# Relu, gate arithmetic and a small product on GpSimd, and a new planned order, in a memory-attention kernel followed by two MLPs

## The chip, the cores and the metric

The kernel runs on one core of one Trainium2 chip. The metric is the device time of one execution in microseconds. The core's engines are TensorE (PE, with its weight loads as PEld), VectorE (DVE), ScalarE (ACT), GpSimd (POOL) and SyncE (SP, which here issues the DMAs). Each engine takes its own queue in the order of the program and waits on semaphores of the others.

## What is computed

```python
def phi(x):
    return np.where(x > 0, x, np.exp(x) - 1.0) + 1.0
# B, H, S, D = 4, 8, 576, 64
a = softmax(causal(q @ k.T / 8)); local = a @ v
mem_out = (phi(q) @ M_prev) / (phi(q) @ z_prev + 1e-6)
g = 1.0 / (1.0 + np.exp(-beta))                 # one per head
x = (g * mem_out + (1 - g) * local)             # to 2304 x 512
h = x @ w_in;   x = (h * tanh(softplus(h))) @ w_out       # 512 -> 2048 -> 512
h = x @ w_in2;  out = (h * sigmoid(h)) @ w_out2
```

All in float32; the weights of the two MLPs come in as float64 and are brought to float32 bit by bit on the chip.

## The kernel before

**Stages.** Heads are taken two at a time: 16 pairs, each with 576 tokens of two heads. A pair has the scores (`s4` to `s0` on PE, blocks of query rows), their masked minimum on DVE (`r..`, line 588), the exponentials on ACT (`e..`, line 615), transposes on PE (`X1`, `X2`, `X3`, `W`, line 486) that ACT and DVE copy out of PSUM (lines 476 and 479), and the products with v and the memory (`Vhi`, `Vlo`, line 692), which DVE scales into `xT` (line 696). Then the two MLPs run over `xT` in 32 visits (a quarter of the hidden units by a block of tokens); their products are PE lines 1000 to 1002 and 1068, with seven products where eight would be usual and each factor split into a high and a low part.

**phi and its use.** For each pair `phu` (line 507, ACT) makes relu(q) in tile `u`, `phn` (line 505, POOL) makes q - relu(q) in `e`, `phe` (506, ACT) its exponential, `phf` (508, POOL) adds the two. `phz` and `phy` (509 and 512, POOL) multiply by z, `phr` (513, DVE) sums over the features into `c`, `phg` (516 and 517, POOL) and `phd` (519, DVE) turn that into the memory's factors, `phq` (520, DVE) multiplies 8 of them by the softmax's row sums `z`, and `phmh`, `phml`, `phm0` (534 and 539, POOL) scale phi by them. `za`, `zd`, `zg`, `n00` (641 to 647, on POOL and DVE) treat the row sums.

**The gate.** `exp` on ACT (line 434), five small operations on DVE (437 to 441), then three kinds of copies on ACT (446 to 452). Once per execution.

**Weights.** A decode job is a load into `stg`, then `abs`, `b0`, `b1`, `b2`, `b3` on 512 columns (lines 804 to 821, DVE but for the first jobs' `abs` on ACT); `hi` and `lo` parts and the sums for the seven products follow. For the first half of the first quarter of hidden units POOL does the subtractions (lines 847, 866, 869).

**The order.** The program doesn't issue these steps in the order of loops. `Steps.plan` is a list scheduler: every step has an engine, a planned duration, its predecessors, a due time, and the buffers that it takes and gives back. It runs a clock, lets each free engine take the ready step with the least lateness, and the order in which it starts them is the order in which the program issues them. `SHIFT` is a table of numbers, one for each kind of step, that are added to the due times; the change calls this "order sought", so they come from a search. So a change of a planned duration or of `SHIFT` moves instructions on every queue, SP's loads among them, without changing one of them.

Of the kernel before, what the change touches and what calls it, by code (L numbers as in the profile page):

```python
# [36 lines left out]
class Steps:  # L37
# [3 lines left out]
    def __init__(self):  # L41
        self.ops = {}
        self.cap = {}
        self.takes, self.gives = {}, {}
        self.order_of = {}
        self.after = {}
        self.lag = {}
        self.cols = {}
        self.shift = {}
        self.mode = {}  # L50

# [21 lines left out]
    def plan(self):  # L73
# [44 lines left out]
        mode = 0  # L118
        passed = {}
        self.start = {}  # L120
        order = []
        while done < len(ops):
# [6 lines left out]
            for e in engs:  # L129
# [3 lines left out]
                while ready[e]:  # L133
# [22 lines left out]
                    if k in self.cols:  # L156
                        cycles, count = self.cols[k]
                        if passed.get(int(now / TICK) - 1, 0.0) < BUSY:
                            d = max(d, cycles / 1200.0)
                        t = now  # L160
                        while t < now + d - 1e-9:
                            q = int(t / TICK + 1e-9)
                            b = min(now + d, (q + 1) * TICK)
                            passed[q] = passed.get(q, 0.0) + count * (b - t) / d
                            t = b
                    self.start[k] = now
# [92 lines left out]
def pair_steps():  # L259
# [4 lines left out]
    E("phu", "A", 0.58, ["ldnq"])  # L264
    E("phn", "G", 1.37, ["phu"])
    E("phe", "A", 0.58, ["phn"])
    E("phf", "G", 1.37, ["phe", "phu"])
# [10 lines left out]
    for i in (4, 3, 2, 1):  # L278
# [17 lines left out]
        if i == 1:  # L296
# [7 lines left out]
            E("phq", "D", 0.12, ["za", "phd"])  # L304
# [34 lines left out]
class Attn:  # L339
# [89 lines left out]
    def gates(self):  # L429
# [5 lines left out]

        def sig():
            nc.vector.tensor_scalar(bt, bt, 1.0, None, op0=ALU.add)
            nc.vector.reciprocal(self.g, bt)
            nc.vector.tensor_scalar(self.g1, self.g, -1.0, 1.0, op0=ALU.mult, op1=ALU.add)
            nc.vector.tensor_scalar(self.g1c, self.g1, 1e-20, None, op0=ALU.max)  # L440
            nc.vector.tensor_tensor(self.btg, self.g1c, bt, op=ALU.mult)
# [11 lines left out]
        return exp, sig, spread  # L453
# [40 lines left out]
    def steps(self, p):  # L494
# [10 lines left out]
        f["phn"] = lambda: nc.gpsimd.tensor_tensor(self.get(p, "e"), s["nq"], s["u"], op=ALU.subtract)  # L505
        f["phe"] = lambda: nc.scalar.activation(s["e"], s["e"], AF.Exp)
        f["phu"] = lambda: nc.scalar.activation(self.get(p, "u"), s["nq"], AF.Relu)
# [4 lines left out]
        f["phy"] = lambda: nc.gpsimd.tensor_tensor(s["u"][:, 8], s["e"][:, 8], self.bt[b]["y"][:, hp], op=ALU.mult)  # L512
# [7 lines left out]
        f["phq"] = lambda: nc.vector.tensor_tensor(s["c"][:, :8], s["c"][:, :8], s["z"][:, :8], op=ALU.mult)  # L520
# [184 lines left out]
    def register(self, m):  # L705
        m.cap.update({"A." + r: c for r, c in self.RINGS.items()})
        m.cap.update({"A." + r: t[4] for r, t in self.TILES.items()})
        exp, sig, spread = self.gates()
        m.add(("gate", "exp"), "A", 0.2, [], exp, 25.0, 5.2)
        m.add(("gate", "sig"), "D", 1.0, [("gate", "exp")], sig, 26.0)  # L710
        m.add(("gate", "spread"), "A", 1.0, [("gate", "sig")], spread, 28.0)
# [54 lines left out]
def ps2(n):  # L766
    return 0.126 + n / 960
# [6 lines left out]
class Weights:  # L774
# [104 lines left out]
    def register(self, m, due, last1, last2):  # L879
        m.cap.update({"W.raw": 2, "W.val": self.VALS})  # L880
        for n, job in enumerate(JOBS):
# [5 lines left out]
            slow = 0.05 if first else 0.0  # L887
            for x, e, d, deps in (("ld", "S", 2.2, []), ("abs", "A", 0.53, ["ld"]) if first else ("abs", "D", 0.465, ["ld"]),
                                  ("b0", "D", 0.465, ["abs"]), ("b1", "D", 0.465, ["b0"]), ("b2", "D", 0.735, ["b1"]),
                                  ("b3", "D", 0.735, ["b2"])):  # L890
                m.add(J(x), e, d + (slow if e == "D" else 0.0), [J(y) for y in deps], f[x], t,
# [10 lines left out]
        for ph in range(2):  # L902
            for pr in range(NF // 2):
# [5 lines left out]
                d2 = lambda n: 0.25 + n / 480 if g == "G" else dve(n)  # L909
# [16 lines left out]
class Moe:  # L926
# [169 lines left out]
    def register(self, m, base, ends):  # L1096
# [38 lines left out]
        for n, ((ph, tp), vs, kind) in enumerate(run):  # L1135
# [5 lines left out]
            if kind == "comp":  # L1141
# [10 lines left out]
                mk = lambda x, e, d, deps, at: m.add(K(x), e, d, deps, f[x], at - 2.0)  # L1152
                mk("T1", "D", D2, [K("l11")], min(need["T1"], need["T2"]))
# [32 lines left out]
        for v, (ph, g, tp) in enumerate(VISITS):  # L1186
            w = TBS[tp]
            for c in range(2):
# [13 lines left out]
                act2 = lambda n, ps: (0.17 if ps else 0.212) + n / 1200  # L1202
# [48 lines left out]
    ('gate', 'exp'): -1546.35, ('gate', 'sig'): -1000.81, ('gate', 'spread'): -1110.7, ('a', 'ldkT'): -1506.04,  # L1251
# [219 lines left out]
```

## Time and profile before

| | us |
|---|---|
| three executions | 950.07, 951.50, 951.98 (median 951.5) |
| span of the profiled execution, first to last instruction | 949.0 |
| PE busy in it | 921.2 (97%) |
| DVE busy | 662.5 (70%) |
| ACT busy | 498.9 (53%) |
| POOL busy | 140.4 (15%) |

The profile is of one execution. Its own device time isn't listed apart from the span; the three listed times lie 1.1 to 3.0 us over the span. Busy shares are means over stages that differ: POOL's 140 us all lie in the first fifth.

### The profile page before, as it was taken

Reading aid. Unit: us, or ns where it says so; the run is one execution under the profiler, and the core shown is the slowest. Engines: PE = TensorE matmul, PEld = TensorE weight load, DVE = VectorE, ACT = ScalarE, POOL = GpSimd, SP = SyncE. Lnnn points to the kernel's source line nnn. Section 1 sums busy time; section 2 is a strip of 40 time slices with the busy share of each in tenths; the row PEclk is TensorE's granted clock in tenths of the full one; section 3 lists DMA queues with packets and bytes.
Section 4 is the critical chain, followed back from the end, with each engine's and each line's share of the span. In section 5 each row is a group of like instructions: output and inputs, shape, how many; then the busy total and the mean of one; then the engine's idle time right before and its main releaser. Section 6 shows DMA issues by size and latency. Waiting matters only on the chain.

```text
span 949.0 us, 17264 instructions
## 1 busy us (share of the span) xinstructions
PE 921.2 (97%) x6544; PEld 813.1 (86%) x6544; DVE 662.5 (70%) x1504; ACT 498.9 (53%) x1172; POOL 140.4 (15%) x223
## 2 busy tenths in 40 slices
PE   4989999999999999999999999999999999999998
PEld 2656666799999999999999999998999888989986
DVE  4899899988984558665957889766647765754333
ACT  5998899876654243433433647554533442433330
POOL 5688798300000000000000000000000000000000
PEclk9999999999999999999999999999999999999999
DMA  6546563666647403850375535704550374024412
GB/s 209 149 158 194 165 199 121 213 261 235 221 150 250 156 1 98 274 156 1 117 253 197 221 119 198 278 23 162 189 177 10 108 265 145 1 93 147 157 54 99
DMA packets 60034, 147.72 MB, mean 156 GB/s; under 512 B 7600, under 2 KB 25136, under 8 KB 59952
## 3 DMA queue, kind: packets, MB, share of 16 engines
q1 hardware_dynamic: 59808, 146.30, 45.4%
q8 instruction: 51, 0.84, 0.4%
q10 hardware_dynamic: 144, 0.33, 0.1%
q14 instruction: 31, 0.25, 0.1%
HBM read 108.79 MB, written 37.81 MB: 154 GB/s over the span
## 4 chain that ended last, share of the span: by engine, by line
PE 85%; DVE 4%; ACT 3%; POOL 3%; issue 2%; DMA 2%; SPq 0%; DVEq 0%; POOLq 0%
PE acc L1068 42%; PE psX L1000 7%; PE psX L1001 7%; PE psX L1002 7%; PE psY L1000 4%; PE psY L1001 4%; PE psY L1002 4%; DVE sm L588 2%; PE psW L1001 2%; PE psW L1002 2%; PE psW L1000 2%; PE ps_t L692 2%; PE ps_s L595 2%; PE ps_t L486 1%; ACT Ph L615 1%
## 5 line engine op out<-in xcount | busy, mean ns | idle before, releaser
L1068 PE MATMUL acc<-g,w 128*128 128x320 f32 (+1 forms) x1152 | 218.3, 337 | 0.0
L1068 PE MATMUL acc<-w,g 128*128 128x512 f32 x864 | 214.4, 394 | 0.0
L1068 PEld LDWEIGHTS acc<-g,w 128*128 128x128 f32 x1152 | 183.8, 188 | 13.1
L1068 PEld LDWEIGHTS acc<-w,g 128*128 128x128 f32 x864 | 157.8, 188 | 30.5
L1031 ACT COPY vt<-psX 128x256 f32<-128x256 f32 (+1 forms) x192 | 75.2, 398 | 154.8 <-PE psX L1002 146.0
L1089 DVE TENSOR_TENSOR xT<-acc,xT 128x512 f32<-128x512 f32 (+1 forms) x126 | 77.2, 613 | 93.8 <-PE acc L1068 92.9
L1041 DVE TENSOR_TENSOR g<-vt,g 128x512 fp32r<-128x512 f32 (+1 forms) x128 | 94.1, 754 | 35.4 <-ACT g L1040 34.7
L1029 DVE TENSOR_TENSOR vt<-psY,vt 128x256 f32<-128x256 f32 (+1 forms) x128 | 57.9, 456 | 87.1 <-ACT vt L1031 46.2
L1040 ACT CAST g<-vt 128x512 fp32r<-128x512 f32 (+1 forms) x128 | 83.4, 672 | 31.5 <-PE acc L1068 30.1
L1000 PE MATMUL psX<-x,w 128*128 128x320 f32 (+1 forms) x256 | 75.8, 296 | 0.0
L1001 PE MATMUL psX<-x,w 128*128 128x320 f32 (+1 forms) x256 | 75.7, 296 | 0.0
L1002 PE MATMUL psX<-x,w 128*128 128x320 f32 (+1 forms) x256 | 75.6, 295 | 0.0
L595 PE MATMUL ps_s<-kT,qT 64*128 64x288 f32 (+3 forms) x320 | 66.8, 480 | 6.3 <-DMA kT<-in_kT_dram 4.6
L1037 ACT ACTIVATE vt<-vt 128x640 f32<-128x640 f32 (+1 forms) x64 | 43.8, 685 | 51.8 <-DVE vt L1029 51.5
L588 DVE CUSTOM_DVE_ANT_0 sm<-ps_s,mask 128x288 f32<-128x288 f32 (+3 forms) x128 | 56.9, 472 | 5.4 <-PE ps_s L595 3.1
L1035 ACT ACTIVATE vt<-vt 128x256 f32<-128x256 f32 (+1 forms) x64 | 28.5, 445 | 59.7 <-DVE vt L1029 59.7
L1036 ACT ACTIVATE vt<-psX 128x256 f32<-128x256 f32 (+1 forms) x64 | 26.0, 407 | 50.2 <-PE psX L1002 50.1
L1029 DVE TENSOR_TENSOR vt<-psW,vt 128x256 f32<-128x256 f32 (+1 forms) x64 | 29.1, 455 | 31.7 <-PE psW L1002 31.2
L1000 PEld LDWEIGHTS psX<-x,w 128*128 128x128 f32 x256 | 48.2, 188 | 2.0 <-issue 0.2
L1001 PEld LDWEIGHTS psX<-x,w 128*128 128x128 f32 x256 | 48.3, 189 | 1.7
L875 ACT CAST w<-val 128x512 fp32r<-128x512 f32 (+1 forms) x64 | 34.8, 567 | 26.5 <-DVE val L866 13.1
L1002 PEld LDWEIGHTS psX<-x,w 128*128 128x128 f32 x256 | 48.3, 188 | 0.0
(126 smaller groups left out, 2019.1 us busy)
## 6 DMA issues: line engine op xcount, KB each, us to landing
stg<-in_moe_w_in_dram SPq DMA_DIRECT2D x32, 512.0 KB, 5.6
stg<-in_moe_w_out_dram SPq DMA_DIRECT2D x32, 512.0 KB, 3.5
x<-sp SPq DMA_DIRECT2D x18, 640.0 KB, 4.2
x<-sp SPq DMA_DIRECT2D x18, 512.0 KB
sp<-x SPq DMA_DIRECT2D x12, 640.0 KB, 2.9
sp<-x SPq DMA_DIRECT2D x12, 512.0 KB, 4.1
nv<-in_v_dram SPq DMA_DIRECT2D x16, 320.0 KB, 4.3
x1T<-sp01T SPq DMA_DIRECT2D x8, 640.0 KB
```

What stands on the lines that cost most here:

```text
L588: nc.vector.tensor_tensor_reduce(out, ps, mask, -0.125, init, ALU.add, ALU.min, acc)
L595: nc.tensor.matmul(ps, lhsT=s["qT"][R[j], qcols(i)], rhs=s["kT"][R[j], k0 + cols.start:k0 + cols.stop], start=True, stop=True)
L1000: nc.tensor.matmul(o, lhsT=W(0, kc), rhs=X(0, kc), start=(n in (1, 2, 7) and kc == 0), stop=False, skip_group_check=True)
L1001: nc.tensor.matmul(o, lhsT=W(0, kc), rhs=X(1, kc), start=False, stop=False, skip_group_check=True)
L1002: nc.tensor.matmul(o, lhsT=W(1, kc), rhs=X(0, kc), start=False, stop=(kc == 1), skip_group_check=True)
L1029: nc.vector.tensor_tensor(o, self.bank[q, to], o, op=ALU.add)
L1031: f[f"s{n}"] = lambda n=n: nc.scalar.copy(val(*at[n]), self.bank[q, "X"])
L1037: f["m2"] = lambda: nc.scalar.activation(val(1), val(1), fn)
L1040: f[f"h{c}"] = lambda c=c: nc.scalar.copy(hi(c), val(c))
L1041: f[f"l{c}"] = lambda c=c: nc.vector.tensor_tensor(self.gt(q, c)[:, 1, :2 * tb], val(c), hi(c).bitcast(F32), op=ALU.subtract)
L1068: nc.tensor.matmul(y, lhsT=a, rhs=b, start=(c == 0 and k == 0), stop=(c == 1 and k == 5))
L1089: nc.vector.tensor_tensor(part, acc, part, op=ALU.add)
```

## The change

Per pair: relu goes to POOL as a `max` with 0; `phn` becomes a `min` with 0 of q itself, so that it no longer waits for relu; `phq` goes from DVE to POOL. Of the gate's five operations on DVE only the reciprocal stays there, the others go to POOL. In the planner, a POOL step and a DVE step of the set `lock` now wait for each other (`lock` holds the decode steps on DVE and the subtractions that split the MLPs' inputs), some planned durations are smaller, and the table `SHIFT` is another one throughout.

```diff
+                    if e == "D" and k in self.lock:
+                        d += max(0.0, port["G"] - now)
+                        port["D"] = now + d
+                    if e == "G":
+                        d += max(0.0, port["D"] - now)
+                        port["G"] = now + d
...
-    E("phu", "A", 0.58, ["ldnq"])
-    E("phn", "G", 1.37, ["phu"])
+    E("phn", "G", 0.9, ["ldnq"])
     E("phe", "A", 0.58, ["phn"])
+    E("phu", "G", 0.9, ["ldnq"])
...
-            E("phq", "D", 0.12, ["za", "phd"])
+            E("phq", "G", 0.22, ["za", "phd"])
...
+        def one():
+            nc.gpsimd.tensor_scalar(bt, bt, 1.0, None, op0=ALU.add)
         def sig():
-            nc.vector.tensor_scalar(bt, bt, 1.0, None, op0=ALU.add)
             nc.vector.reciprocal(self.g, bt)
-            nc.vector.tensor_scalar(self.g1, self.g, -1.0, 1.0, op0=ALU.mult, op1=ALU.add)
-            nc.vector.tensor_scalar(self.g1c, self.g1, 1e-20, None, op0=ALU.max)
-            nc.vector.tensor_tensor(self.btg, self.g1c, bt, op=ALU.mult)
+        def rest():                # the same three on nc.gpsimd
...
-        f["phn"] = lambda: nc.gpsimd.tensor_tensor(self.get(p, "e"), s["nq"], s["u"], op=ALU.subtract)
+        f["phn"] = lambda: nc.gpsimd.tensor_scalar(self.get(p, "e"), s["nq"], 0.0, None, op0=ALU.min)
-        f["phu"] = lambda: nc.scalar.activation(self.get(p, "u"), s["nq"], AF.Relu)
+        f["phu"] = lambda: nc.gpsimd.tensor_scalar(self.get(p, "u"), s["nq"], 0.0, None, op0=ALU.max)
-        f["phq"] = lambda: nc.vector.tensor_tensor(s["c"][:, :8], s["c"][:, :8], s["z"][:, :8], op=ALU.mult)
+        f["phq"] = lambda: nc.gpsimd.tensor_tensor(s["c"][:, :8], s["c"][:, :8], s["z"][:, :8], op=ALU.mult)
...
-    ... "abs", "D", 0.465 ... "b0" 0.465, "b1" 0.465, "b2" 0.735, "b3" 0.735 (+ 0.05 for the first jobs)
+    ... "abs", "D", 0.335 ... "b0" 0.335, "b1" 0.335, "b2" 0.6, "b3" 0.6, all in m.lock
...
 SHIFT = {                       # every number another
-    ('gate', 'exp'): -1546.35, ('gate', 'sig'): -1000.81, ('gate', 'spread'): -1110.7,
+    ('gate', 'exp'): -2090.82, ('gate', 'one'): 3021.36, ('gate', 'sig'): 731.24, ('gate', 'rest'): 1.31,
```

## Rows read from the trace of the kernel before

**Rows 1.** Busy time by stage (windows): length, then each engine's, PEclk, DMA, GB/s.
```profile
core 0: us, PE busy (x) PEld busy (x) DVE busy (x) ACT busy (x) POOL busy (x), PEclk, DMA share, GB/s
...
14.00:182.00 168.00, 156.43 (x1815) 105.70 (x1816) 152.50 (x544) 154.26 (x472) 132.05 (x208) 0.98 0.52 163
78.00:80.00 2.00, 2.00 (x20) 1.34 (x20) 2.00 (x5) 0.62 (x3) 1.83 (x3) 0.50 0.50 192
106.00:108.00 2.00, 2.00 (x18) 1.17 (x16) 1.44 (x4) 1.66 (x4) 1.75 (x5) 0.50 0.92 217
182.00:946.00 764.00, 762.52 (x4724) 706.11 (x4722) 506.94 (x956) 341.13 (x694) 1.80 (x1) 1.00 0.44 152
```
**Rows 2.** What PE waited for, whole span (waits): us in total, times, longest.
```profile
PE ps_s L634 <- DVE m L588: 7.8, 2, 7.6
PE ps_s L595 <- DMA kT<-in_kT_dram: 4.6, 1, 4.6
```
**Rows 3.** The first 15 us (timeline): start, length, instruction.
```profile
4.05 0.60 SPq L461 DMA_DIRECT2D nq<-in_q_dram  x1
...
4.65 2.29 PE L595 MATMUL ps_s<-kT,qT 64*128 64x288 f32 x8 [4.65 <-DMA kT<-in_kT_dram]
...
6.15 0.68 ACT L507 ACTIVATE u<-nq 128x576 f32<-128x576 f32 x1 [3.92 <-DMA nq<-in_q_dram]
...
10.08 0.68 ACT L507 ACTIVATE u<-nq 128x576 f32<-128x576 f32 x1 [3.25 <-DMA nq<-in_q_dram]
10.66 0.19 ACT L434 ACTIVATE bt<-bt 128x8 f32<-128x8 f32 x1
...
10.84 1.40 POOL L505 TENSOR_TENSOR e<-nq,u 128x576 f32<-128x576 f32 x1 [2.47 <-ACT u L507]
10.89 1.37 DVE L437 TENSOR_SCALAR bt<-bt 128x8 f32<-128x8 f32 x1 [10.03 <-ACT bt L434]
...
13.98 0.46 DVE L588 CUSTOM_DVE_ANT_0 sm<-ps_s,mask 128x288 f32<-128x288 f32 x1
```
**Rows 4.** A relu on ACT and the instruction after it (timeline).
```profile
23.41 0.68 ACT L507 ACTIVATE u<-nq 128x576 f32<-128x576 f32 x1
...
23.98 0.78 ACT L615 ACTIVATE Ph<-sm,m 128x576 f32<-128x576 f32 x1
```
**Rows 5.** DVE from 14 to 182 us by shape (groups): busy, mean ns, idle before.
```profile
L520 DVE TENSOR_TENSOR c<-c,z 128x8 f32<-128x8 f32 x16 | 7.1, 444 | 0.0
L821 DVE SCALAR_TENSOR_TENSOR val<-stg,val 128x512 uint32<-128x512 uint32 x7 | 6.3, 896 | 0.1
L814 DVE TENSOR_SCALAR val<-val 128x512 f32<-128x512 f32 x8 | 6.0, 754 | 1.7 <-ACT val L804 1.7
```
**Rows 6.** The same lines on DVE from 182 to 946 us, where POOL is idle (groups).
```profile
L821 DVE SCALAR_TENSOR_TENSOR val<-stg,val 128x512 uint32<-128x512 uint32 x57 | 38.7, 685 | 0.5
...
L814 DVE TENSOR_SCALAR val<-val 128x512 f32<-128x512 f32 x56 | 24.2, 441 | 0.5
```
**Rows 7.** Line 520 alone: ns shortest, median, longest (source).
```profile
L520 DVE TENSOR_TENSOR c<-c,z x16: 101/298/1201, 24.3 to 174.8; 128x8 f32<-128x8 f32 x16
```
**Rows 8.** POOL's groups over the whole span: busy, mean ns, idle before.
```profile
L505 POOL TENSOR_TENSOR e<-nq,u 128x576 f32<-128x576 f32 x16 | 22.8, 1422 | 6.5 <-ACT u L507 6.2
...
L517 POOL TENSOR_TENSOR c<-c,bt 128x9 f32<-128x9 f32 x16 | 3.3, 204 | 1.3
...
L420 POOL TENSOR_SCALAR_AFFINE_SELECT smask<-smask 64x64 f32<-64x64 f32 x2 | 0.5, 234 | 0.1
...
L413 POOL TENSOR_SCALAR_AFFINE_SELECT mask<-mask 128x128 f32<-128x128 f32 x1 | 0.3, 292 | 0.1
```
**Rows 9.** POOL's two kinds of tensor_scalar: ns shortest, median, longest (source).
```profile
L516 POOL TENSOR_SCALAR c<-c x16: 201/202/569, 20.7 to 170.2; 128x9 f32<-128x9 f32 x16
L647 POOL TENSOR_SCALAR P<-P,r,g1s x16: 440/452/964, 24.5 to 175.0; 128x128 f32<-128x128 f32 x16
```
**Rows 10.** What POOL waited for from 14 to 182 us (waits).
```profile
POOL e L508 <- ACT e L506: 11.6, 7, 2.9
...
POOL P L647 <- DVE c L520: 3.8, 5, 1.2
```
**Rows 11.** The end of the attention stage (timeline): POOL's last step, the first MLP matmul.
```profile
177.07 1.28 POOL L847 TENSOR_TENSOR w<-val,w 128x512 fp32r<-128x512 f32 x1
...
181.64 0.39 PE L1000 MATMUL psX<-x,w 128*128 128x256 f32 x1
```
**Rows 12.** Decode steps on DVE back to back (timeline).
```profile
188.06 0.42 DVE L806 TENSOR_SCALAR val<-stg 128x512 uint32<-128x512 uint32 x1
188.40 0.68 DVE L818 SCALAR_TENSOR_TENSOR val<-stg,val 128x512 uint32<-128x512 uint32 x1
189.00 0.81 DVE L964 TENSOR_TENSOR x<-xT,x 128x640 fp32r<-128x640 f32 x1
```

More of the change, by code (lines that the diff above doesn't have):

```diff
@@ L50, in __init__ @@
         self.mode = {}
+        self.lock = set()
     def add(self, name, eng, dur, deps, fn, due, after=0.0, lag=0.0, cols=None):
@@ L118, in plan @@
         mode = 0
+        port = {"D": 0.0, "G": 0.0}
         passed = {}
@@ L434, in exp @@
             nc.scalar.activation(bt, bt, AF.Exp, scale=-1.0)
+        def one():
+            nc.gpsimd.tensor_scalar(bt, bt, 1.0, None, op0=ALU.add)
         def sig():
-            nc.vector.tensor_scalar(bt, bt, 1.0, None, op0=ALU.add)
             nc.vector.reciprocal(self.g, bt)
-            nc.vector.tensor_scalar(self.g1, self.g, -1.0, 1.0, op0=ALU.mult, op1=ALU.add)
-            nc.vector.tensor_scalar(self.g1c, self.g1, 1e-20, None, op0=ALU.max)
-            nc.vector.tensor_tensor(self.btg, self.g1c, bt, op=ALU.mult)
+        def rest():
+            nc.gpsimd.tensor_scalar(self.g1, self.g, -1.0, 1.0, op0=ALU.mult, op1=ALU.add)
+            nc.gpsimd.tensor_scalar(self.g1c, self.g1, 1e-20, None, op0=ALU.max)
+            nc.gpsimd.tensor_tensor(self.btg, self.g1c, bt, op=ALU.mult)
         def spread():
@@ L452, in spread @@
                 nc.scalar.copy(self.g1s[r, :], gv[r, j, :])
-        return exp, sig, spread
+        return exp, one, sig, rest, spread
     def load(self, p, nm, queue=None):
@@ L511, in steps @@
             self.bt[b]["z"][:, h0:h0 + 2, :].unsqueeze(1).to_broadcast([P, 4, 2, D]), op=ALU.mult)
-        f["phy"] = lambda: nc.gpsimd.tensor_tensor(s["u"][:, 8], s["e"][:, 8], self.bt[b]["y"][:, hp], op=ALU.mult)
+        f["phy"] = lambda: nc.gpsimd.tensor_tensor(self.get(p, "u")[:, 8], s["e"][:, 8], self.bt[b]["y"][:, hp], op=ALU.mult)
         f["phr"] = lambda: nc.vector.tensor_reduce(out=self.get(p, "c"), in_=s["u"], axis=AX.X, op=ALU.add)
@@ L707, in register @@
         m.cap.update({"A." + r: t[4] for r, t in self.TILES.items()})
-        exp, sig, spread = self.gates()
+        exp, one, sig, rest, spread = self.gates()
         m.add(("gate", "exp"), "A", 0.2, [], exp, 25.0, 5.2)
-        m.add(("gate", "sig"), "D", 1.0, [("gate", "exp")], sig, 26.0)
-        m.add(("gate", "spread"), "A", 1.0, [("gate", "sig")], spread, 28.0)
+        m.add(("gate", "one"), "G", 0.2, [("gate", "exp")], one, 25.5)
+        m.add(("gate", "sig"), "D", 0.12, [("gate", "one")], sig, 26.0)
+        m.add(("gate", "rest"), "G", 0.6, [("gate", "sig")], rest, 27.0)
+        m.add(("gate", "spread"), "A", 0.75, [("gate", "rest")], spread, 28.0)
         for p in range(B * NP):
@@ L766, in ps2 @@
 def ps2(n):
-    return 0.126 + n / 960
+    return 0.07 + n / 960
 def sb1(n):
@@ L886, in register @@
             first = self.first(job)
[L887 to L891, printed above, removed]
+            for x, e, d, deps in (("ld", "S", 2.2, []), ("abs", "A", 0.57, ["ld"]) if first else ("abs", "D", 0.335, ["ld"]),
+                                  ("b0", "D", 0.335, ["abs"]), ("b1", "D", 0.335, ["b0"]), ("b2", "D", 0.6, ["b1"]),
+                                  ("b3", "D", 0.6, ["b2"])):
+                if e == "D":
+                    m.lock.add(J(x))
+                m.add(J(x), e, d, [J(y) for y in deps], f[x], t,
                       lag=1.6 if x == "ld" else 0.0, after=20.0 + 20.0 * n if first and x == "ld" else 0.0)
@@ L908, in register @@
                 g = "G" if ph == 0 and pr < GC // 2 else "D"
-                d2 = lambda n: 0.25 + n / 480 if g == "G" else dve(n)
+                d2 = lambda n: 0.18 + n / 480 if g == "G" else dve(n)
                 t = max(due[a], due[b])
@@ L1152, in register @@
                 mk = lambda x, e, d, deps, at: m.add(K(x), e, d, deps, f[x], at - 2.0)
+                m.lock.update(K(x) for x in ["l" + x for x in XOPS] + ["T1", "T2", "T3", "T4"])
                 mk("T1", "D", D2, [K("l11")], min(need["T1"], need["T2"]))
@@ L1201, in register @@
                     last1.setdefault((ph, pr), []).append(N(n))
-                act2 = lambda n, ps: (0.17 if ps else 0.212) + n / 1200
+                act2 = lambda n, ps: (0.067 if ps else 0.108) + n / 1200
                 e = due[N(4)] + 4.0
@@ L1250 @@
 SHIFT = {
-    ('gate', 'exp'): -1546.35, ('gate', 'sig'): -1000.81, ('gate', 'spread'): -1110.7, ('a', 'ldkT'): -1506.04,
[100 rows of a table removed]
+    ('gate', 'exp'): -2090.82, ('gate', 'one'): 3021.36, ('gate', 'sig'): 731.24, ('gate', 'rest'): 1.31,
[93 rows of a table added]
 }
```

193 rows, old and new, of the table SHIFT are left out of this document.

## The prediction

> **What bounds the kernel now.** I first read the page's slices and then cut the span at the stages. [...] So the span is the attention stage, some 182 us, plus a fixed 764 us, plus 3 us for the last drain and store. What the attention stage gives up, the kernel gives up one for one.
>
> The second reading is that stage. From 14 to 182 us, 168 us, DVE is busy 152.5 (91%), ACT 154.3 (92%), POOL 132.1 (79%), and PE 156.4 (93%) [rows 1]. [...] No engine is alone the bound: four queues run almost full, and each waits a little for the others. Relief of one of them is worth less than its own time.
>
> The third is the start. Of what PE waited for, the two longest entries are one wait of 7.6 us before line 634 for DVE, and the first load [rows 2]. The timeline shows why: PE has its first scores by 4.65 + 2.29 = 6.94 us, but DVE takes up the first of them only at 13.98. Until then DVE stands at the gate's first operation, which waits for ACT's `exp` at 10.66, which stands in ACT's queue behind the relu of pair 1, which waits for its q until 10.08 (its load was issued at 4.05). Then the gate's five operations take 3.1 us, since the first, on 8 elements, takes 1.37 us beside POOL's 1.40 us line 505 [rows 3].
>
> **The change part by part.**
>
> ACT loses 16 relus. One is 0.68 us long, but the next instruction on ACT starts 23.98 - 23.41 = 0.57 us after it [rows 4], so 16 x 0.57 = 9.1 us leave ACT's queue.
>
> DVE loses 16 times line 520, mean 444 ns, 7.1 us busy [rows 5]. It works on 8 elements and takes 101 ns at its shortest, 1201 at its longest [rows 7]; the rest is a wait inside the instruction. Taking 0.07 us off each for the overlap with its follower, 16 x 0.374 = 6.0 us leave DVE's queue.
>
> DVE's decode steps show the same wait: line 814 takes 754 ns in this stage against 441 where POOL is idle, line 821 896 against 685 [rows 5, 6]. With lines 816 and 818, which lie between them, I put the 29 such steps of the stage at about 29 x 0.22 = 6.4 us of waiting. The new planner knows of it and may place them better, but POOL also gets more to do. Bounds: 6.4 us gained, or 1 lost (POOL's busy share rises from 79% to at most 151 / 164 = 92%, and this waiting by the same sixth); I take 1.5 gained. The planner's new durations (0.335 and 0.60) are nearer to the chip than the old 0.465 and 0.735: the decode steps start 0.34 and 0.60 us apart [rows 12].
>
> [...]
>
> POOL loses 16 x 1.42 = 22.8 us of `phn` [rows 8], and gets 32 one-input operations on 576 elements, 16 `phq` and four gate operations. `phq` and a gate operation have their like in line 517, 0.20 us on 9 elements [rows 8]: 20 x 0.21 = 4.2 us. The one-input operation isn't in this trace at that size. From below: the affine select takes 234 ns on 64 and 292 on 128 elements [rows 8], which goes on to 0.292 + 448 x 0.00091 = 0.70 us. From above: line 647, a tensor_scalar with two operands per partition, takes 452 ns on 128 against 202 for line 516 on 9 [rows 9], 2.1 ns an element, which goes on to 1.39 us, as dear as a two-input operation (1.42). I take 0.9, the planner's number, since constants instead of operands per partition make it more like the select. Then POOL's work is 140.4 - 22.8 + 28.8 + 4.2 = 150.6 us; with 0.70 it is 144.2, with 1.39 it is 166.3.
>
> [...]
>
> Waits that go: `phn` no longer stands behind relu on another engine (6.2 us of POOL's idle time [rows 8]); relu can now fill the gap in which POOL waits for the exponential (11.6 us), and POOL no longer waits for line 520 (3.8 us) [rows 10]. These 21.6 us of idle time are what lets POOL carry 10 us more. Waits that come: the relus and `phq` now stand in POOL's queue ahead of `phf`, `phz` and the scaling, and PE's transposes `W` and `X3` wait for that scaling.
>
> The lock terms, the durations and `SHIFT` change no instruction. I cost them by what the order can reach.
>
> **The sum.** Start: with the gate's arithmetic off DVE, and its steps given late due times in place of early ones, the first scores can be taken at about 6.94 instead of 13.98 us: at most 7.0 us. Pair 0 gives DVE some 5 us of work (11 instructions of line 588 of about 0.46 us [rows 3]); by then pair 1's q has landed, since its relu starts at 10.08 now. ACT and POOL start up in the same chain, so I take 5.0 of the 7.0 us; the lower bound is nothing, if something else stands at the head of DVE's queue.
>
> Steady part: ACT falls from 154.3 to 145.2 and DVE from 152.5 to 152.5 - 6.0 - 1.5 = 145.0 us. At the share of 92% that they hold now, 168 us would become 158. But PE's 156.4 us would then be 99% of it, and POOL's would be about 143 of it, where it now has 132. I let PE reach 95.5%: 156.4 / 0.955 = 164, a gain of 4.0 us. Bounds: nothing, and 10.
>
> MLP stage: 0, with 0 to 3 us lost as bounds, since 1.5 us of idle PE time is all there is to gain, and any gap counts in full.
>
> Span 949.0 - 5.0 - 4.0 = 940.0. The median of the runs is 951.5, 2.5 us over the span, so 942.5 us.
>
> **The rivals.**
>
> *POOL becomes the bound (slower).* Place: the one-input operations on POOL, at 1.39 us as line 647 suggests. POOL's 166.3 us at the 92% that the full queues hold need 180.8 us from its first phi step, which starts at 6.15 at the earliest, and end at 187; now its last step ends at 177.07 + 1.28 = 178.4 [rows 11]. That is 8.6 us later, and the first MLP matmul (181.64 [rows 11]) with it: 960. It decides where POOL's work is over 0.92 x (178.4 - 6.15) = 158.5 us, that is at 1.15 us an operation. For it: line 647, and the two-input operations. Against it: the select. 13%.
>
> [...] A decode step on DVE that meets a POOL operation waits, now 0.22 us on average [rows 5, 6]. If each of the 29 waited through a whole 0.9 us operation, DVE would have 152.5 - 6.0 + 29 x 0.68 = 166.2 us to do, at 92% 181 us, 13 more than the stage has now; less the start's 5 the time would be 959.5. It decides where the waits grow by 0.44 us each. [...] With a planner that models such waits it is unlikely: 6%.
>
> *Only a part (faster by little).* PE is the bound of the steady part, or the start's gain is filled by the next wait there (pair 1's loads, ACT's first exponentials): 2 to 4 us, 948.5. 16%.
>
> *Nothing.* The new order puts another waiting step in front of DVE's first score, and the saved time of ACT and DVE becomes idle time behind PE and POOL: 949.6 to 953.4. 10%.
>
> **Chances and range.** The forecast, 4 to 16 us faster, has 55%: 935.5 to 947.5, with 942.5 the likeliest by the sum. 0.2% is 1.9 us, about what a measurement can tell from no change here (the three runs lie 1.9 apart). Faster: 55 + 16 = 71%; the same 10%; slower 13 + 6 = 19%. The range for 8 in 10 runs from 935 (the start's 7 and the steady part's 10 us, almost in full) to 954, over the case of nothing and the smaller losses. It leaves out about 16% above and 4% below.
>
> **What would show it.** Right: the first instruction of line 588 starts at 6 to 9 us and PE's long wait before line 634 is gone; relu and `phn` on POOL take 0.7 to 1.0 us; ACT's busy time falls by about 11 us and DVE's by about 9 over the whole span; the first MLP matmul stands at about 172 us; PE is busy over 99.5% from there on. Wrong: those operations take over 1.15 us and PE waits for POOL's scaling; lines 814 to 821 grow longer in the attention stage; DVE's first score again stands behind the gate or a phi step; or PE shows idle time after 190 us.

## The result: slower, and the profile after

| | us |
|---|---|
| before, median of 4 executions | 951.74 (950.07 to 953.51) |
| after, median of 4 executions | 960.76 (959.76 to 960.99) |
| ratio | 1.0095 (95%: 1.008 to 1.011) |

The change costs 9.0 us; 942.5 was forecast, 9 us less than before. The profiled execution of after took 960.99 us, 1.9 more than its span. The head of its page, span and busy time of the engines:

```profile
span 959.1 us, 17228 instructions
...
PE 928.5 (97%) x6544; PEld 814.6 (85%) x6544; DVE 647.6 (68%) x1484; ACT 493.0 (51%) x1158; POOL 172.2 (18%) x259
```

Against the table of before, ACT gave up 5.9 us (the forecast had about 11) and DVE 14.9 (about 9), the two that the change was to relieve, and POOL took up 31.8 where the forecast had 10. After's windows by stage, with the columns of [rows 1]:

```profile
14.00:182.00 168.00, 151.34 (x1710) 99.42 (x1710) 138.29 (x504) 142.76 (x446) 158.63 (x237) 0.98 0.50 156
...
192.00:956.00 764.00, 761.59 (x4703) 703.81 (x4701) 498.44 (x952) 340.35 (x694) 1.30 (x1) 1.00 0.43 151
```

From 14 to 182 us POOL is the fullest queue, 158.6 us (94%) where it had 132.1 [rows 1], and DVE (82%) and ACT (85%) have room that they don't use. The MLP stage looks much as before, with PE busy for 761.6 of 764 us (762.5 [rows 1]), only 10 us later. After's groups on POOL (and ACT's exponential between them; busy, mean ns of one, idle before) say what fills POOL:

```profile
L519 POOL TENSOR_SCALAR u<-nq 128x576 f32<-128x576 f32 x16 | 26.9, 1679 | 6.1 <-DMA nq<-in_q_dram 5.2 <-DVE c L525 1.0
...
L517 POOL TENSOR_SCALAR e<-nq 128x576 f32<-128x576 f32 x16 | 26.3, 1648 | 0.2
...
L520 POOL TENSOR_TENSOR e<-e,u 128x576 f32<-128x576 f32 x16 | 22.8, 1423 | 1.1 <-ACT e L518 1.1
...
L518 ACT ACTIVATE e<-e 128x576 f32<-128x576 f32 x16 | 10.9, 683 | 14.2 <-POOL e L517 14.2
```

Relu (L519) and the minimum (L517) take 1.65 to 1.68 us each, more than a two-input operation on the same tile (1.42), and 53.2 us in place of the 28.8 of the sum. The wait has turned round too: ACT now idles 14.2 us for L517, where POOL idled 11.6 for ACT's exponential [rows 10]; that entry of POOL is down to 1.1.

The end of the attention stage, after's timeline (start, length, instruction), answers to [rows 11]:

```profile
185.24 1.28 POOL L861 TENSOR_TENSOR w<-val,w 128x512 fp32r<-128x512 f32 x1
...
187.62 0.39 PE L1015 MATMUL psW<-x,w 128*128 128x256 f32 x1
...
192.68 1.68 PE L704 MATMUL ps_t<-h,nv 128*64 128x256 f32 x16
```

POOL's last step of the stage ends at 186.52 us against 178.35 [rows 11], 8.2 later, and PE's last product with v starts at 192.68 against 184.47, 8.2 later too; the first MLP matmul, which runs between, is 6.0 later. Before's last product with v:

```profile
184.47 1.68 PE L692 MATMUL ps_t<-h,nv 128*64 128x256 f32 x16
```

The 8.2 us are most of the span's 10.1. The other 1.9 lie behind that product: from its start to the end of the span after takes 766.4 us, before 764.5. One piece of it shows where the first MLP goes over to the second. There the new order has ACT load its function tables three times within 12 us (lines 1050, 1052 and 1051, 1.28 us each), where before does it once, and PE waits for ACT; two lines of after's timeline:

```profile
565.69 1.28 ACT L1051 ACT_TABLE_LOAD   x1
...
565.73 0.41 PE L1015 MATMUL psX<-x,w 128*128 128x320 f32 x1 [0.56 <-ACT vt L1046]
```

The rest of the 1.9 us wasn't followed.

The start, which was to gain 5 us, in after's timeline:

```profile
6.18 1.66 POOL L519 TENSOR_SCALAR u<-nq 128x576 f32<-128x576 f32 x1 [2.94 <-DMA nq<-in_q_dram]
6.99 0.46 DVE L600 CUSTOM_DVE_ANT_0 sm<-ps_s,mask 128x288 f32<-128x288 f32 x1 [6.13 <-PE ps_s L607]
...
10.07 1.65 POOL L519 TENSOR_SCALAR u<-nq 128x576 f32<-128x576 f32 x1 [2.24 <-DMA nq<-in_q_dram]
11.69 3.26 POOL L517 TENSOR_SCALAR e<-nq 128x576 f32<-128x576 f32 x2
...
14.91 0.25 POOL L445 TENSOR_SCALAR bt<-bt 128x8 f32<-128x8 f32 x1
...
15.19 0.20 DVE L448 RECIPROCAL g<-bt 128x8 f32<-128x8 f32 x1 [6.34 <-POOL bt L445]
```

DVE takes up its first scores at 6.99 us, as forecast (13.98 before [rows 3]). But 2 us later it stands at the gate's reciprocal for 6.34 us: the addition in front of it (L445) now stands in POOL's queue behind pair 1's relu, which waits for its q until 10.07, and two minima, 3.26 us. PE's longest wait for DVE is 5.1 us instead of 7.6, but the sum of these waits is 8.1 us against 7.8 [rows 2]:

```profile
PE ps_s L646 <- DVE m L600: 8.1, 5, 5.1
```

### The profile page after: what moved, and what is told of

It reads as the page before. It is cut to its first block, busy times and chain, and to the rows that moved or that the text cites. A ratio compares the mean times of both kernels' runs of the same rounds, so it can differ in the third digit from the quotient of the medians.

```text
span 959.1 us, 17228 instructions
## 1 busy us (share of the span) xinstructions
PE 928.5 (97%) x6544; PEld 814.6 (85%) x6544; DVE 647.6 (68%) x1484; ACT 493.0 (51%) x1158; POOL 172.2 (18%) x259
## 4 chain that ended last, share of the span: by engine, by line
PE 82%; POOL 4%; DVE 1%; ACT 1%; issue 1%; DMA 1%; SPq 0%; DVEq 0%; POOLq 0%; ACTq 0%
PE acc L1083 41%; PE psX L1015 7%; PE psX L1016 7%; PE psX L1017 7%; PE psY L1015 4%; PE psY L1016 4%; PE psY L1017 4%; PE psW L1015 2%; PE psW L1016 2%; PE psW L1017 2%; PE ps_t L704 1%; PE ps_s L607 1%; POOL u L519 1%; PE ps_t L498 1%; DMA R<-rd 1%
## 5 line engine op out<-in xcount | busy, mean ns | idle before, releaser
L1083 PE MATMUL acc<-g,w 128*128 128x320 f32 (+1 forms) x1152 | 212.9, 337 | 0.0
L1083 PE MATMUL acc<-w,g 128*128 128x512 f32 x864 | 208.7, 394 | 0.0
L607 PE MATMUL ps_s<-kT,qT 64*128 64x288 f32 (+3 forms) x320 | 70.9, 491 | 6.8 <-DMA kT<-in_kT_dram 4.6
L1015 PE MATMUL psX<-x,w 128*128 128x256 f32 (+1 forms) x256 | 76.3, 298 | 0.6 <-ACT vt L1046 0.6
L1016 PE MATMUL psX<-x,w 128*128 128x256 f32 (+1 forms) x256 | 75.7, 296 | 0.0
L1017 PE MATMUL psX<-x,w 128*128 128x256 f32 (+1 forms) x256 | 75.6, 295 | 0.0
L1052 ACT ACTIVATE vt<-vt 128x512 f32<-128x512 f32 (+1 forms) x64 | 43.9, 686 | 51.2 <-DVE vt L1044 51.2
L600 DVE CUSTOM_DVE_ANT_0 sm<-ps_s,mask 128x192 f32<-128x192 f32 (+3 forms) x128 | 57.2, 472 | 17.1 <-PE ps_s L607 10.0
L607 PEld LDWEIGHTS ps_s<-kT,qT 64*128 64x128 f32 x320 | 35.1, 207 | 16.1 <-DVE m L600 6.7
L627 ACT ACTIVATE Ph<-sm,m 128x576 f32<-128x576 f32 (+1 forms) x64 | 46.0, 719 | 3.8 <-DVE m L600 3.8
L889 ACT CAST w<-val 128x512 fp32r<-128x512 f32 (+1 forms) x64 | 34.9, 565 | 21.3 <-DVE val L880 15.0
L1051 ACT ACTIVATE vt<-psX 128x320 f32<-128x320 f32 (+1 forms) x64 | 26.1, 407 | 36.9 <-PE psX L1017 36.6
```

The source lines that it names most:

```text
L600: nc.vector.tensor_tensor_reduce(out, ps, mask, -0.125, init, ALU.add, ALU.min, acc)
L607: nc.tensor.matmul(ps, lhsT=s["qT"][R[j], qcols(i)], rhs=s["kT"][R[j], k0 + cols.start:k0 + cols.stop], start=True, stop=True)
L627: nc.scalar.activation(ptile(i)[:, o:o + w] if i else G("P0")[:, 2], s[f"sm{i}{j}"], AF.Exp, bias=s[f"m{i}"][:, j:j + 1], scale=-1.0, accu ...
L1015: nc.tensor.matmul(o, lhsT=W(0, kc), rhs=X(0, kc), start=(n in (1, 2, 7) and kc == 0), stop=False, skip_group_check=True)
L1016: nc.tensor.matmul(o, lhsT=W(0, kc), rhs=X(1, kc), start=False, stop=False, skip_group_check=True)
L1017: nc.tensor.matmul(o, lhsT=W(1, kc), rhs=X(0, kc), start=False, stop=(kc == 1), skip_group_check=True)
```

## The experiments

The theory at the outset: the forecast's one wrong step is the price of the operation (1.65 instead of 0.9 us), and POOL has become the bound. The rivals: the new order itself is bad; the price is a wait beside DVE's work, not the operation's own; what DVE and ACT lose was worth nothing anyway.

**1. Relu back on ACT, in after's order.** POOL loses 16 of the 32 operations.

```diff
-        f["phu"] = lambda: nc.gpsimd.tensor_scalar(self.get(p, "u"), s["nq"], 0.0, None, op0=ALU.max)
+        f["phu"] = lambda: nc.scalar.activation(self.get(p, "u"), s["nq"], AF.Relu)
```

> The changed kernel with every queue's order kept, but relu issued on ACT again (the min stays on POOL, the gate's arithmetic and the small product too). It takes 16 x 1.65 = 26 us out of POOL's 172 and puts 16 x 0.57 = 9 us back on ACT. Theory 1 (POOL's work bounds the attention stage, the order is fine): POOL's 146 us no longer bound it, the stage ends 10 to 18 us earlier than in the changed kernel and the time is 943 to 951, at or below the kernel before. Theory 2 (the new order is itself worse on the chip, whatever the engine of relu): the time stays at 956 to 962. [...]

Measured: 951.74 us (950.22 to 954.26), ratio to before 1.0003 (0.999 to 1.0016). POOL is busy 146.8 us instead of 172.2, and the whole loss is gone. That lies just over the 943 to 951 of the first theory, and outside the 956 to 962 of the second. The order, the gate's new place, the minimum and `phq` on POOL are all still in; so they are not the loss, and together they are no gain either while ACT keeps the relus.

**2. Both operations as two-input additions of a tile of zeros.** Same engine, same order, the price 1.42 instead of 1.65; the clamping by minimum and maximum is left out, here and in experiment 3.

```diff
-        f["phu"] = lambda: nc.gpsimd.tensor_scalar(self.get(p, "u"), s["nq"], 0.0, None, op0=ALU.max)
+        f["phu"] = lambda: nc.gpsimd.tensor_tensor(self.get(p, "u"), s["nq"], self.zero, op=ALU.add)
...                                # phn likewise
```

> The changed kernel in the same order, with both one-input operations replaced by a two-input add of zeros of the same size on POOL (left out: the clamping by min and max, so the values aren't phi's). The kernel before shows such an operation at 1.42 us against 1.65 for the new one-input one, so POOL's work falls by 32 x 0.23 = 7.4 us. Theory 1 (POOL's work is the bound, one for one): 952 to 955. Theory 2 (order): within 1.5 us of the changed kernel, 959 to 962.

Measured: 956.97 us (956.74 to 958.51), ratio 1.0059 (1.004 to 1.0078). POOL's busy time is 165.7, 6.5 less than after's, and the time 3.8 less. The time follows POOL's work, but it lies between the two expected ranges: not one for one, as the first theory had it (952 to 955), and not unmoved (959 to 962).

**3. Both operations as products with two columns of ones**, a form that takes nearly what the planner assumes.

```diff
-        f["phu"] = lambda: nc.gpsimd.tensor_scalar(self.get(p, "u"), s["nq"], 0.0, None, op0=ALU.max)
+        f["phu"] = lambda: nc.gpsimd.tensor_scalar(self.get(p, "u"), s["nq"], self.one, self.one, op0=ALU.mult, op1=ALU.mult)
...                                # phn likewise
```

> The changed kernel in its own order, with both operations replaced by a POOL operation of the same size that was measured alone at 0.82 us (a product with two per-partition ones; left out: the clamping, so the values aren't phi's). That is the nearest to the planner's 0.9, so this is the change as it was planned, with its order. POOL's work falls from 172 to about 146 us, and ACT keeps its relief. Theory 1 (the step that failed is the operation's price, all else of the forecast holds): 940 to 946. Theory 1b (POOL was the bound, but the order gives no more than the old one even at its own costs): 948 to 952. Theory 2 (order bad on the chip): 955 or more.

Measured: 945.13 us (943.51 to 947.8), ratio 0.9936 (0.9912 to 0.9959). The groups of this run:

```profile
L519 POOL TENSOR_SCALAR u<-nq,one 128x576 f32<-128x576 f32 x16 | 13.8, 865 | 8.1 <-DMA nq<-in_q_dram 5.9 <-DVE c L525 2.2
...
L517 POOL TENSOR_SCALAR e<-nq,one 128x576 f32<-128x576 f32 x16 | 13.2, 826 | 0.2
```

At 0.83 to 0.87 us an operation, with nothing else changed, the change is 6.1 us faster than before, by the ratio, as the first theory had it. POOL's work of 172.2, 165.7 and 148.0 us gives 960.8, 957.0 and 945.1: 0.58 and 0.67 us of time for each us of POOL (0.53 and 0.66 by the ratios to before). So the loss grows about evenly over these three; no edge shows at which POOL begins to bound. One window from 20 to 170 us, first of after, then of this run (columns as in [rows 1]):

```profile
20.00:170.00 150.00, 136.82 (x1538) 89.30 (x1537) 123.22 (x453) 126.06 (x391) 141.56 (x210) 0.98 0.52 163
```

```profile
20.00:170.00 150.00, 142.86 (x1707) 95.96 (x1704) 132.63 (x489) 134.29 (x420) 131.79 (x230) 0.97 0.55 169
```

Relieved of 9.8 us, POOL lets the other three do 6 to 9 us more in the same stretch. PE's share is 95.2%; the forecast had put 95.5%. DVE's busy time over the whole span is 644.0 us against after's 647.6, so longer waits of DVE beside POOL can be only a small part of the 15.6 us between the two kernels.

Experiment 1 against 3 also prices ACT's relus: POOL is equally full (146.8 and 148.0 us), ACT has 9.5 us less to do, and the ratios lie 0.0067 apart, some 6.4 us (3.8 to 9.0 by their intervals). The two kernels also differ in which steps make up POOL's work, so this is a price from one pair of kernels.

**4. The planner told the truth**, after's kernel with `SHIFT` as it is.

```diff
-    E("phn", "G", 0.9, ["ldnq"])
+    E("phn", "G", 1.62, ["ldnq"])
-    E("phu", "G", 0.9, ["ldnq"])
+    E("phu", "G", 1.62, ["ldnq"])
```

> The changed kernel's program with only the planner's duration of the two operations on POOL set from 0.9 to the measured 1.62 us; the table SHIFT is not searched anew, so the order is the one that this table gives under true costs. POOL's work is the same 172 us. Theory 1 (load): POOL still can't end before about 185 us, and the time is 956 to 964. Theory 2 (the order made under a wrong duration is what costs): a good part of the 9 us comes back, 950 to 955.

Measured: 974.2 us (973.7 to 975.25), ratio 1.0242 (1.0225 to 1.0259), 13 us worse than after, and outside both expected ranges. The instructions are the same, in another order; so the order is the cause, and this table of due times, sought for one set of durations, doesn't fit the other. One place, in this run's timelines of POOL and PE:

```profile
71.63 0.72 POOL L880 TENSOR_TENSOR val<-val 128x256 f32<-128x256 f32 x1
72.31 2.93 POOL L880 TENSOR_TENSOR w<-val,w 128x512 fp32r<-128x512 f32 x2
75.21 1.06 POOL L546 TENSOR_TENSOR Ph<-e,c 128x256 f32<-128x256 f32 x1
76.23 0.20 POOL L656 TENSOR_TENSOR rx<-r,g1c 128x8 f32<-128x8 f32 x1
...
76.49 0.08 PEld L577 LDWEIGHTS ps_t<-ident,rx 128*8 128x8 f32 x1 [3.75 <-POOL rx L656]
```

PE waits 3.75 us for `rx`, 0.20 us of work on 8 elements, which the order has put behind three of the weights' subtractions (L880) and a scaling on POOL (the matmul behind this weight load names ACT's cast L889 for its wait, which ended 0.02 us after `rx`). This wait cost more than its own length. Windows of this run, the whole stage (columns as in [rows 1]) and then PE alone (busy, PEclk, DMA, GB/s):

```profile
14.00:182.00 168.00, 148.83 (x1645) 98.70 (x1647) 141.74 (x489) 137.94 (x429) 155.33 (x226) 0.93 0.52 158
```

```profile
74.00:76.00 2.00, 0.00 (x0) 0.50 0.05 17
...
80.00:82.00 2.00, 2.00 (x12) 0.50 0.82 269
```

PE's granted clock fell to 0.50 in the wait and was still there four us after PE had work again: eight products with v (L704, 128x256) took 1.52 us from 80.12, where after's eight at a granted clock of 1.00 took 0.82 (from 189.83). Over the stage the clock is 0.93 where after has 0.98: by an estimate from these two means, some 17 us more at 0.50, or up to 8 us of PE's work at 1.00. Not every us of the 13 was followed like this.

**5. The gate's exponential first, in before's kernel**, to price the start by itself.

```diff
-        for k in self.plan():
+        order = self.plan()
+        order.remove(("gate", "exp"))
+        order.insert(order.index((0, "phu")), ("gate", "exp"))
+        for k in order:
```

> The kernel before with one instruction moved on one queue: the gate's exp on ACT stands ahead of pair 0's relu, and so no longer behind pair 1's. Every other queue is as before. DVE's first score should start at about 7 us and not at 13.98. If what the start gives arrives at the end (my forecast's 5 us of 7): 944 to 948. If the stage's later waits fill it: 950 to 952, no change.

Measured: 948.77 us (946.06 to 952.91), ratio 0.9974 (0.9959 to 0.999): 2.5 us (1.0 to 3.9), between the two expected ranges. Timeline of this run:

```profile
5.57 0.17 DVE L440 TENSOR_SCALAR bt<-bt 128x8 f32<-128x8 f32 x1 [4.71 <-ACT bt L437]
...
7.06 0.46 DVE L591 CUSTOM_DVE_ANT_0 sm<-ps_s,mask 128x288 f32<-128x288 f32 x1 [0.47 <-PE ps_s L598]
...
12.31 0.23 DVE L591 CUSTOM_DVE_ANT_0 sm<-ps_s,smask 128x64 f32<-128x64 f32 x1 [3.38 <-PE ps_s L637]
```

The gate's operations, with POOL idle beside them, take 0.17 to 0.20 us, where the first took 1.37 [rows 3]. DVE is at its scores at 7.06, and out of work from 8.9 to 12.3, since PE waits for pair 1's k until then:

```profile
PE ps_s L637 <- DMA kT<-in_kT_dram: 3.7, 1, 3.7
```

So the first score comes 6.9 us earlier, DVE stands idle for 3.4 of them until the next load is in, and 2.5 arrive at the end.

**6. `phq` alone on POOL, in before's kernel.**

```diff
-        f["phq"] = lambda: nc.vector.tensor_tensor(s["c"][:, :8], s["c"][:, :8], s["z"][:, :8], op=ALU.mult)
+        f["phq"] = lambda: nc.gpsimd.tensor_tensor(s["c"][:, :8], s["c"][:, :8], s["z"][:, :8], op=ALU.mult)
```

> The kernel before with only the product of the memory's factors with the row sums on POOL, at the same place of the order. 7.1 us of busy time leave DVE, most of it waiting, and 3.3 us go to POOL. By my sum's 6 us on DVE, if DVE's queue alone set the pace: 946 to 949. If the stage is bound by several queues at once: 950 to 952.

Measured: 950.89 us (947.8 to 954.29), ratio 0.9992 (0.9976 to 1.0008): no difference that can be told. What leaves DVE (6.0 us by the forecast; its busy time falls by 4.4, from 662.5 to 658.1) is worth under 2.3 us by itself.

**7. The operations one by one, on POOL alone.** Nothing of the kernel is in it: one tile of 128x576 is loaded, and each operation runs twice with the other engines idle.

```python
G.tensor_scalar(o, x, 0.0, None, op0=ALU.max)                            # L53; min L54, add L55, mult by 1.0 L56
G.tensor_scalar(o, x, 1.0, 0.0, op0=ALU.mult, op1=ALU.add)               # L57
G.tensor_scalar(o, x, 0.0, 1.0, op0=ALU.max, op1=ALU.min)                # L58
...
G.tensor_scalar(o, x, c[:, 0:1], c[:, 1:2], op0=ALU.mult, op1=ALU.mult)  # L60
G.tensor_tensor(o, x, y, op=ALU.add)                                     # L61
```

> Not the kernel: POOL alone runs its operations one after another on a 128 x 576 tile and smaller ones, and VectorE and ScalarE one relu each; the output is zeros. [...] The slope over 64, 128, 288 and 576 columns gives ns an element. If add or mult with a constant takes about 0.7 to 0.9 us at 576, the planner's 0.9 holds for another operation and max and min are the dear ones; if all take 1.4 to 1.7, one-input work on POOL is as dear as two-input work.

Timeline of this run (max on 64 elements is L66, a copy L68, a max on DVE L69):

```profile
3.64 1.65 POOL L53 TENSOR_SCALAR o<-x 128x576 f32<-128x576 f32 x1 [3.21 <-DMA x<-in_q_dram]
5.37 1.65 POOL L54 TENSOR_SCALAR o<-x 128x576 f32<-128x576 f32 x1
7.10 1.66 POOL L55 TENSOR_SCALAR o<-x 128x576 f32<-128x576 f32 x1
8.85 1.65 POOL L56 TENSOR_SCALAR o<-x 128x576 f32<-128x576 f32 x1
10.58 0.67 POOL L57 TENSOR_SCALAR o<-x 128x576 f32<-128x576 f32 x1
11.34 2.14 POOL L58 TENSOR_SCALAR o<-x 128x576 f32<-128x576 f32 x1
...
15.40 0.82 POOL L60 TENSOR_SCALAR o<-x,c 128x576 f32<-128x576 f32 x1
16.31 1.40 POOL L61 TENSOR_TENSOR o<-x,y 128x576 f32<-128x576 f32 x1
...
22.62 0.36 POOL L66 TENSOR_SCALAR o<-x 128x64 f32<-128x64 f32 x1
...
23.60 0.66 POOL L68 COPY o<-x 128x576 f32<-128x576 f32 x1
24.30 0.46 DVE L69 TENSOR_SCALAR y<-o 128x576 f32<-128x576 f32 x1 [22.30 <-POOL o L68]
```

A `max` takes 1.65 us with nothing beside it: the price is the operation's own, not a wait beside DVE's work. From 64 to 576 elements it grows by 1.29 us, 2.5 ns an element. `min`, `add` and `mult` alone cost the same; a product with an addition costs 0.67, and a copy 0.66.

**8. Is there a cheap form of relu on POOL?** Again only such operations, as pairs with a neutral second one.

```python
G.tensor_scalar(o, x, 0.0, 1.0, op0=ALU.max, op1=ALU.mult)    # L53; mult, max L54
...
G.tensor_scalar(o, x, 1.0, 1.0, op0=ALU.mult, op1=ALU.mult)   # L57
G.tensor_scalar(o, x, 0.0, 0.0, op0=ALU.add, op1=ALU.add)     # L58
G.tensor_scalar(o, x, 0.0, 1.0, op0=ALU.add, op1=ALU.mult)    # L59
```

> Not the kernel: POOL alone on a 128 x 576 tile, tensor_scalar with two operations in one instruction, to see which pairs are cheap (the output is zeros). The first such run showed 0.67 us for a product and a sum with constants, 0.82 us for two products with per-partition operands, and 1.65 us for any single operation. Theory A (a cheap routine exists for products and sums only, in pairs): max or min beside a neutral product or sum stays at 1.6 us or more, and relu can't be made cheap on POOL this way. Theory B (the cheap routine is for any two operations of which one is a product or a sum): max then times 1 takes 0.67 to 0.9 us, and the change can be mended by writing relu and min so.

Timeline of this run:

```profile
3.67 2.13 POOL L53 TENSOR_SCALAR o<-x 128x576 f32<-128x576 f32 x1 [3.25 <-DMA x<-in_q_dram]
...
12.55 0.67 POOL L57 TENSOR_SCALAR o<-x 128x576 f32<-128x576 f32 x1
13.31 2.15 POOL L58 TENSOR_SCALAR o<-x 128x576 f32<-128x576 f32 x1
15.54 0.67 POOL L59 TENSOR_SCALAR o<-x 128x576 f32<-128x576 f32 x1
```

No pair with a `max` or `min` is cheap (2.13 to 2.29 us). Fast are the pairs of products, and of a sum and a product; two sums are not.

**9. Relu on DVE (0.46 us alone), in after's order**, the minimum as q - relu(q) on POOL again and the gate's arithmetic on DVE right behind its exponential.

```diff
-        f["phn"] = lambda: nc.gpsimd.tensor_scalar(self.get(p, "e"), s["nq"], 0.0, None, op0=ALU.min)
+        f["phn"] = lambda: nc.gpsimd.tensor_tensor(self.get(p, "e"), s["nq"], s["u"], op=ALU.subtract)
-        f["phu"] = lambda: nc.gpsimd.tensor_scalar(self.get(p, "u"), s["nq"], 0.0, None, op0=ALU.max)
+        f["phu"] = lambda: nc.vector.tensor_scalar(self.get(p, "u"), s["nq"], 0.0, None, op0=ALU.max)
...                                # phu put ahead of phn, the gate's three steps behind its exp
```

> A mended version in the changed kernel's order: relu on DVE as a max with 0 (a 128 x 576 operation there was measured alone at 0.46 us), phn on POOL as the subtraction of before (1.42 us), directly behind relu; the gate's arithmetic on DVE directly behind exp, where DVE is idle; the small product stays on POOL. POOL's work is 172 - 53 + 23 = 142 us, ACT keeps its 9 us of relief, DVE gets some 6 us more than in the changed kernel. If POOL's load was all that was wrong with the change, and DVE has room: 944 to 949. If DVE's added work and waits cost what the relief gave: 950 to 954.

Measured: 952.18 us (950.4 to 954.02), ratio 1.0007 (0.9996 to 1.0019): no gain, the second of the two expected cases. POOL has 144.1 us of work here, less than in experiment 3, but DVE has 657.9, which is 13.9 more: relief of POOL alone was not enough here. What DVE's added work costs, and what the minimum's wait for relu costs, wasn't tried apart.

**10. The same two operations, the gate as in the change, and an order sought anew** for durations read from the traces and for the times at which the first loads land.

```diff
-    E("phn", "G", 0.9, ["ldnq"])
+    E("phu", "D", 0.37, ["ldnq"])
+    E("phn", "G", 1.37, ["phu"])
-    E("phu", "G", 0.9, ["ldnq"])
...                                # phu and phn as in experiment 9
+                aft = {(0, 'ldnq'): 1.2, (1, 'ldnq'): 6.2, (1, 'ldqT'): 7.7, (1, 'ldkT'): 8.5}.get((p, n), 0.0)
...                                # SHIFT: every number another
```

> Relu on DVE, phn as the subtraction on POOL, the gate's arithmetic and the small product on POOL as in the change, and the order sought anew with the durations that the chip shows (relu 0.37 us on DVE's queue, phn 1.37, and the first loads landing when they do in the trace). If the sum of forecast holds once the prices are right: 942 to 947, below the kernel before. If the planner still misses what limits the stage, 949 to 955.

Measured: 946.79 us (946.11 to 950.24), ratio to before 0.9956 (0.9941 to 0.9972), 4.2 us faster than before by the ratio, and some 13 than after, as the first case had it. Window of this run:

```profile
20.00:170.00 150.00, 143.22 (x1710) 95.89 (x1712) 143.48 (x505) 135.72 (x423) 131.61 (x214) 1.00 0.56 172
```

POOL and ACT are about as full as in experiment 3 (131.8 and 134.3), DVE carries the relus, and PE gets the same 95%. Between 9 and 10 lie 5.4 us, for the new order and the gate's other place together; they weren't tried apart.

## Why the prediction was wrong

**The failed step is one price:** "I take 0.9, the planner's number, since constants instead of operands per partition make it more like the select." The operation takes 1.65 us. POOL's work is 172.2 us instead of the sum's 150.6, past the point (158.5, or 1.15 us an operation) from which the first rival was to decide. That rival is what happened: it gave 960, and after takes 960.8. Experiments 2 and 3, which change only this price (and leave out the clamping), take the loss back step by step. The rival's form was too sharp: the runs show some 0.6 us of time for each us of POOL and no edge, where it had nothing up to 158.5 us and one for one from there.

**Why the bounds didn't hold it.** 0.70 to 1.39 came from a select and from the two lines of [rows 9]. Those two are both of the cheap kind that experiments 7 and 8 found: line 516 is a product with an addition, line 647 two products. The step from 202 to 452 ns was taken as 2.1 ns an element. An estimate from experiment 7 and line 516 is 0.15 us for operands per partition (0.82 against 0.67) and 0.83 ns an element ((0.67 - 0.20) / 567): 0.20 + 0.15 + 119 x 0.00083 = 0.45 us on 128 elements, as the two products of experiment 7 took there (0.45). So the upper bound was wrong for line 647's own form (0.82 at 576 elements), and said nothing of a single `max`. No row of before showed one at any large size: the honest range was wider, and 13% for the rival too little.

**The rival's own size was right by luck.** With 1.65 in its formula POOL has 140.4 - 22.8 + 52.8 + 4.2 = 174.6 us, which at 92% from 6.15 us would end at 196, not at 186.5. The formula counted against that stretch about 3 us of POOL's set-up before 6 us, and 92% where POOL held 93 to 94%; the rest of POOL's operations came out 2.8 us cheaper (119.0 instead of 121.8). The too low 1.39 made up for these.

**The steady part was sound in the main.** Given nearly the planned price (experiment 3; POOL has 148.0 us there, the sum 150.6), PE's share came to 95.2% (95.5 forecast) and the time to 945.1 against 942.5. The first MLP matmul came at 173.04 us (172 forecast), but that sign flatters: the new order starts it 5.1 us ahead of the last product with v, the old one 2.8. ACT's 9.1 us are the part that counts (6.4 us, experiments 1 and 3); DVE's 6.0 of `phq` alone count for nothing measurable (experiment 6).

**The start was mis-sized:** 5.0 of 7.0 us taken, 2.5 measured by itself (experiment 5). "By then pair 1's q has landed" looked at the wrong load: pair 1's k lands last, at some 12 us, and DVE has only 1.9 us of work before that in experiment 5, not the 5 of the sum. In after much of this was given back, by the gate's addition behind phi steps on POOL; the prediction had named such a wait as a way to be wrong. PE's busy time in the first 20 us (windows, columns as in [rows 1]) of before, of after and of experiment 3:

```profile
0.00:20.00 20.00, 7.78 (x45) 4.95 (x47) 7.41 (x29) 8.95 (x25) 10.74 (x18) 1.00 0.59 205
```

```profile
0.00:20.00 20.00, 9.29 (x52) 6.35 (x53) 5.20 (x26) 8.13 (x26) 13.86 (x23) 1.00 0.60 201
```

```profile
0.00:20.00 20.00, 11.52 (x66) 8.13 (x68) 6.64 (x32) 9.99 (x33) 12.95 (x27) 1.00 0.70 234
```

By this measure after is 1.5 us ahead of before at 20 us, and experiment 3 is 3.7. Experiment 3's span is 4.9 us shorter than before's (944.1 and 949.0): some 3.7 from the start, 1.5 lost behind the last product with v (766.0 us against 764.5), and so some 2.7 from the steady part, where 4.0 was forecast. No one term parts it from the forecast; the split is an estimate, since busy time isn't work done.

**DVE's waits beside POOL were a small term, and so was their rival.** Decode steps in the stage, after's groups from 14 to 182 us:

```profile
L828 DVE TENSOR_SCALAR val<-val 128x512 f32<-128x512 f32 x7 | 5.8, 835 | 0.0
...
L835 DVE SCALAR_TENSOR_TENSOR val<-stg,val 128x512 uint32<-128x512 uint32 x6 | 5.2, 860 | 0.1
...
L830 DVE TENSOR_SCALAR val<-val 128x512 uint32<-128x512 uint32 x7 | 3.4, 493 | 0.0
```

Before they took 754, 896 and 615 ns [rows 5 for the first two]: one waits longer, two less, and in sum almost nothing moves (the fourth kind, L832, takes 875 ns after 841). With the shorter operations of experiment 3 they take 542, 738 and 620: POOL's longer operations do lengthen DVE's, but with the fourth kind (875 and 700 ns) by some 3 us in all. 1.5 us of gain was taken; the 0.44 us each, from which these waits would have decided, is far off. That each step waits through a whole operation of POOL, the 0.68 us more behind that rival's 959.5, is shown by no run: after's four means lie between 0.12 us under and 0.08 over before's.

**The MLP stage** was put at 0 with 0 to 3 us lost as bounds, from PE's 762.5 busy of 764 us at a granted clock of 1.00 [rows 1]; by the 766.4 us against 764.5 behind the last product with v, the new order loses 1.9 there. **Open:** where these come from but for the 0.6 us of one wait, and why the order of experiment 4 loses all of its 13 us, of which one place was read.

## What to carry to other kernels

An operation that the trace doesn't show at the size and in the form in question has no price: measure it by itself before it is put 32 times on a queue, since a bound drawn from another form can lie on the wrong side. Moving work off two full queues onto a third pays only as long as the third stays light enough: here, between 148 and 172 us of work on POOL, each us there cost about 0.6 us of time. Durations given to a planner and the order sought for them belong together: corrected durations under the old table were worse than wrong ones, and an order sought anew, with relu on DVE, beat both kernels.

## What the runs showed of the hardware

GpSimd's `tensor_scalar` on 128x576 float32 showed three prices in experiments 7 and 8: 0.67 us for a pair of products or of a sum and a product (0.82 with two operands per partition), 1.65 for each single operation tried with a constant (`max`, `min`, `add`, `mult`), and 2.13 to 2.29 for every other pair tried. So a product alone (1.65) costs more than a product with an addition of 0 (0.67), and more than a two-input operation (1.40). The same `max` on DVE takes 0.46, the relu on ACT 0.68. In experiment 4 a wait of PE cost twice: the granted clock fell to 0.50 while PE waited (3.75 us), and was still 0.50 four us behind the wait, where eight products took 1.52 us that took 0.82 in after at 1.00.
